# Attention's loads cut into pieces of 0.27 MB behind fixed places in TensorE's work, and row stores spread over several steps

## The chip, the cores and the metric

The kernel runs on one core of a Trainium2 chip. The metric is the device time of one execution, in microseconds (us). Before the change three runs gave a median of 729.78 us (729.25 to 739.17).

## The reference

Windowed attention with a few global tokens, followed by a mixture of experts in which a token may stay with the expert of the token before it. All data are fp32. Shapes: batch 8, 8 heads, 512 local and 32 global tokens, head size 64; 8 experts, 512 to 1024 to 512. Cut to what matters:

```python
# attention, for each batch and head
out_g = softmax(q_g @ [k_g, k_l].T / 8) @ [v_g, v_l]            # global tokens see all
s_ll  = where(|i - j| <= 32, q_l @ k_l.T / 8, -1e9)              # local tokens see a window
out_l = softmax([q_l @ k_g.T / 8, s_ll]) @ [v_g, v_l]            # and the global tokens
x = concat([out_g, out_l]) as [8, 576, 512]                      # heads side by side

# mixture of experts, for each batch b and token s in order
fresh = argmax(x[b, s] @ w_gate)
e = fresh if s == 0 or sigmoid(x[b, s] @ w_local) < 0.5 else e_of_the_token_before
p = softmax(x[b, s] @ w_gate)
out[b, s] = p[e] * (relu(x[b, s] @ w1[e]) @ w2[e])
```

## The kernel before

The program has two phases on one core. Attention comes first, in 48 steps; it writes each token's row (512 values, the 8 gate probabilities, the token's number) to a buffer `xs` in HBM. The experts follow: rows are gathered by expert, and two layers of matmuls run on blocks of 256 rows.

In attention a unit is either local, `l` (a pair of heads of one batch), or global, `g` (the global tokens of two pairs). A batch is six units: l, l, g, l, g, l. Step `s` does the scores of unit `s` (`l_s`, `l_max`, `l_exp`, or `g_s`, `g_max`, `g_exp`) and the rest of unit `s - 2`: `l_t` transposes the probabilities on TensorE and ScalarE copies them out of PSUM, `l_av` multiplies them with the values; `g_t` and `g_av` do the same for global units. A few pieces of a finished batch's routing (`f1` to `f3`) are put into later steps, and a list of small VectorE operations drips in between. The order of every engine's instructions is the order in which this code is written; nothing reorders it. In the program's lines: L240 are the local scores, L257 the transposes with the copies L259, L271 the products with the values; L291, L323 and L334 are the same for global units, L347 the transposes of `f1`, L370 a small product of `f2g`.

The loads of attention are issued on SyncE (SP), in order. One pair of heads needs one load of queries and keys (`qk`, 128 partitions, 528 KB) and one of values (`vw`, 128 partitions, 1040 KB), and a batch one small load of global queries (`qg`, 128 KB). The tiles come from rings: 8 for `qk`, 7 for `vw`. In the step of a local unit the kernel asks for the `qk` of the pair five ahead (AHEAD) and the `vw` of the pair four ahead (AHEADV). A load then waits on SP only until its tile is free, that is until the pair that was in it has been used, and everything behind it on SP waits too. GpSimd's `prep` builds a rearranged copy of a pair's keys one local unit ahead (L194).

A batch's rows are stored on ScalarE's queue (ACT) by `f4`, two steps after its routing is done: one store of 512 rows (`xa`, 1056 KB), four of the global tokens' rows (`xg`, 16 KB each) and one of their tail (`gx`, 2 KB), six issues in a row at the start of a step (L407, L411, L412). The stores of the seventh batch come behind the last step, those of the eighth in a list of work that runs beside the first experts' matmuls.

SP's and ACT's transfers share eight completion counters, which the order prints as DMAHW0 to DMAHW7: a transfer that takes a counter first waits for the transfer that had it before.

Four steps before the end of attention the experts' phase begins to work into it (`moe.pre`): the first rows are gathered, and the first expert weights are loaded on SP from step 45 on.

Of the kernel before, what the change touches and what calls it, by code (L numbers as in the profile page):

```python
# [18 lines left out]
P = 128  # L19
B, H, SL, SG, D = 8, 8, 512, 32, 64  # L20
# [34 lines left out]
RE = 2  # L55
XPM = (2, 4, 5, 6)
STORE = 2
AHEAD = 5
AHEADV = 4


def col(b):
# [38 lines left out]
class Attn:  # L101
    def __init__(self, tc, cst, tl, at1, at2, raw, ps, qk, qg, vw, xs):
        nc = self.nc = tc.nc
        self.tc, self.cst = tc, cst
        self.at1, self.at2 = at1, at2
        self.qk, self.qg, self.vw, self.xs = qk, qg, vw, xs
        self.ld = raw
        self.ps_s, self.ps_t, self.ps_o = ps
        self.xa = ring(tl, [P, 4, ROW], F32, "xa", 2)
        self.xa.t.append(at2.tile([P, 4, ROW], F32, name="xa2"))  # L110
        self.xg = ring(tl, [P, 2, D], F32, "xg", 3)
        self.xT = tl.tile([P, 4, SL], F32, name="xT")
# [12 lines left out]
        self.kx = ring(at2, [P, 9, 3, 32], F32, "kx", NBUF)  # L125
        self.pg = ring(at2, [P, 6, P], F32, "pg", NPG)
        self.ptg = ring(at2, [P, 6, P], F32, "ptg", 2)
        self.qgb = ring(at2, [P, NP, 2, 32], F32, "qgb", 2)
        self.mask = at2.tile([P, 4, 2, 32], BF16, name="mask")
        self.m0 = at2.tile([P, 2, 32], F32, name="m0")  # L130
        self.cur = {}
        self.stores = []
        self.s = 0
        self.gens = []
        self.low = 0
        self.banks = False
        self.npr = 0
# [28 lines left out]
    def setup(self):  # L166
# [5 lines left out]
        yield  # L172
        nc.sync.dma_start(self.xs[0:P], zr)

    def load(self, b, pr):
        nc = self.nc
        if pr == 0:
            self.cur[b] = {"v": []}
        c = self.cur[b]
        t = c[("qk", pr)] = self.ld()  # L180
        nc.sync.dma_start(t, self.qk[b, pr])

    def load_g(self, b):
        g = self.cur[b]["qg"] = self.qgb()
        self.nc.sync.dma_start(g, self.qg[b])

    def loadv(self, b, pr):
        nc = self.nc
        v = self.v()
        self.cur[b]["v"].append(v)  # L190
        nc.sync.dma_start(v.rearrange("p w c -> p (w c)"), self.vw[b, pr])

    def cp(self, out, in_, pat):
        self.nc.gpsimd.affine_select(out=out, in_=in_, pattern=pat, compare_op=ALU.is_ge, fill=0.0, base=0, channel_multiplier=0)  # L194
# [26 lines left out]
    def l_s(self, st):  # L221
        nc = self.nc
        b, pr = st["u"]
        if pr == 0:
            self.cur[b]["xa"] = self.xa()
            self.cur[b]["xg"] = self.xg()
        st["pe"] = self.pe()
        q = self.cur[b][("qk", pr)]
        kf = st["kx"].rearrange("p m c k -> p (m c k)")
        sp = st["sp"] = [self.bank(self.ps_s) for _ in range(2)]  # L230
        for h in range(2):
            mo = sp[h].rearrange("p t (k c) -> p t k c", c=32)[:, :, 0::3, :]
            nc.tensor.matmul(mo, self.cst.idb, self.mask, start=True, stop=False, skip_group_check=True)
        for t in range(4):
            for h in range(2):
                r = slice(64 * h, 64 * h + 64)
                for w4 in range(4):
                    w = 4 * t + w4
                    f = 32 * (3 * (w // 2) + w % 2)
                    nc.tensor.matmul(sp[h][32 * w4:32 * w4 + 32, t], q[r, 32 * w:32 * w + 32], kf[r, f:f + P], start=False, stop=True, skip_group_check=True)  # L240

    def l_max(self, st, h):
        nc = self.nc
# [9 lines left out]
    def l_t(self, st, hb):  # L253
        nc = self.nc
        tp = self.bank(self.ps_t)
        for i in range(4):
            nc.tensor.transpose(tp[:, i], st["pe"][:, 4 * hb + i], self.cst.idf)  # L257
        pt = self.pt()
        nc.scalar.copy(out=pt.rearrange("p t w q -> p t (w q)"), in_=tp)  # L259
        st["pts"] = st.get("pts", []) + [pt]  # L260

    def l_av(self, st, h):
        nc = self.nc
        b, pr = st["u"]
        c = self.cur[b]
        v = c["v"][pr]
        pt = st["pts"][h]
        o = self.ps_o()[:, 0:4 * (D + 1)].rearrange("p (t c) -> p t c", c=D + 1)
        for t in range(4):
            for w4 in range(4):  # L270
                nc.tensor.matmul(o[32 * w4:32 * w4 + 32, t], pt[:, t, w4, :],  # L271
                                 v[:, 4 * t + w4, h * (D + 1):(h + 1) * (D + 1)], start=True, stop=True, skip_group_check=True)
        rs = self.rs()
        nc.vector.tensor_scalar(out=rs, in0=o[:, :, D:D + 1], scalar1=1e-9, scalar2=None, op0=ALU.add)
        self.drip(hold=True)
        nc.vector.reciprocal(out=rs, in_=rs)
        self.drip(hold=True)
        n = D * (2 * pr + h)
        nc.vector.tensor_tensor(out=c["xa"][:, :, n:n + D], in0=o[:, :, 0:D], in1=rs.broadcast_to([P, 4, D]), op=ALU.mult)

    def g_s(self, st):
        nc = self.nc
        b, pp = st["u"]
        c = self.cur[b]
        st["sp"] = []
        for n0, n1 in ((0, 256), (256, 544)):
            sp = self.ps_s()
            for i in range(2):
                pr = 2 * pp + i
                k = c[("qk", pr)][:, SL:]  # L290
                nc.tensor.matmul(sp[64 * i:64 * i + 64, 0:n1 - n0], c["qg"][:, pr], k[:, n0:n1], start=True, stop=True, skip_group_check=True)  # L291
            st["sp"].append(sp[:, 0:n1 - n0])

    def g_max(self, st):
        nc = self.nc
# [21 lines left out]
    def g_t(self, st):  # L317
        nc = self.nc
        pt = st["pt"] = self.ptg()
        for c0 in (0, 3):  # L320
            tp = self.bank(self.ps_t)
            for i in range(3):
                nc.tensor.transpose(tp[:, i], st["pg"][:, c0 + i], self.cst.idf)  # L323
            nc.scalar.copy(out=pt[:, c0:c0 + 3], in_=tp[:, 0:3])

    def g_av(self, st):
        nc = self.nc
        b, pp = st["u"]
        c = self.cur[b]
        op = self.ps_o()  # L330
        for ci, w in enumerate(GCH):
            for i in range(4):
                pr, h = 2 * pp + i // 2, i % 2
                nc.tensor.matmul(op[32 * i:32 * i + 32, 0:D + 1], st["pt"][:, ci, 32 * i:32 * i + 32],  # L334
                                 c["v"][pr][:, w, h * (D + 1):(h + 1) * (D + 1)], start=(ci == 0), stop=(ci == 5), skip_group_check=True)
        rs = self.rsg()
        nc.vector.tensor_scalar(out=rs, in0=op[:, D:D + 1], scalar1=1e-9, scalar2=None, op0=ALU.add)
        self.drip(hold=True)
        nc.vector.reciprocal(out=rs, in_=rs)
        self.drip(hold=True)  # L340
        nc.vector.tensor_scalar(out=c["xg"][:, pp], in0=op[:, 0:D], scalar1=rs, scalar2=None, op0=ALU.mult)
# [58 lines left out]
    def f4(self, b, rt):  # L400
# [3 lines left out]
        hf, b4 = b // 4, b % 4  # L404
        rq = slice(32 * b4, 32 * b4 + 32)
        r0 = P * (1 + col(b))
        nc.scalar.dma_start(self.xs[r0:r0 + 4 * P].rearrange("(t p) r -> p t r", p=P), xa)  # L407
        r0 = P * (1 + gcol(hf)) + 32 * b4
        xsg = self.xs[r0:r0 + 32]
        for h in range(4):  # L410
            nc.scalar.dma_start(xsg[:, 0:DM].rearrange("q (a h d) -> q a h d", a=2, h=4)[:, :, h], xg[32 * h:32 * h + 32])  # L411
        nc.scalar.dma_start(xsg[:, DM:ROW], rt.gx[rq])  # L412

    def run(self, rt, moe):
        order = []
# [19 lines left out]
        for k in range(1, AHEAD):  # L435
# [3 lines left out]
                self.load_g(b)  # L439
            if k <= AHEADV:  # L440
                self.loadv(*pairs[k - 1]["u"])
        self.cst.ident()
        warm = self.ps_o()[:, 0:P]
        for _ in range(8):
# [8 lines left out]
        for s in range(n):  # L453
# [30 lines left out]
            else:  # L484
                self.g_s(nx)
                self.g_max(nx)
            fpiece()
            if nl:
                self.l_exp(nx, 0)
            else:  # L490
# [27 lines left out]
        self.drip(1000)  # L518
        for _, b in self.stores:
            self.f4(b, rt)  # L520
        moe.tail = self.tail(units[n - 2], units[n - 1], fin, rt, moe)

    def tail(self, sg, sl, fin, rt, moe):
# [32 lines left out]
        yield  # L556
        yield from rt.stage_b(self.ps_t, self.ps_o, rt.probs(b, c["L"], c["xa"]))
        self.f4(b, rt)
        yield from every(rt.lists(self.ps_o), 2)
        yield LISTS  # L560
        yield from every(rt.kinds(), 3)
# [1018 lines left out]
```

## Time and profile before

| | |
|---|---|
| median of three runs | 729.78 us |
| the profiled execution, a run of its own | 738.59 us |
| its span, first to last instruction | 736.9 us, mean granted TensorE clock 0.959 |
| scores of step 0 begin | 4.80 us |
| scores of the last step (47) begin | 262.76 us |
| the 48 steps and the flush behind them, to | 277.43 us |
| PE busy in 0 to 277 us | 219.61 us, clock 0.91 |
| DVE, ACT, POOL busy there | 182.53, 131.60, 58.76 us |
| bytes moved in those 277 us | 65.46 MB, mean 236 GB/s |

"PE" is TensorE's matmuls, "PEld" its weight loads, which overlap them; "DVE" is VectorE, "POOL" GpSimd, "SPq" and "ACTq" issues of transfers on the queues of SP and ACT. In a wait, the name behind the arrow is what the engine waited for last; "issue" means that nothing which the profile shows was missing.

### The profile page before, as it was taken

How to read it: one execution, taken by the hardware profiler on the slowest of the kernel's cores; microseconds unless marked ns; L12 is line 12 of the kernel's file. 1: busy time of each engine (PE TensorE's matmuls, PEld its weight loads, DVE VectorE, ACT ScalarE, POOL GpSimd, SP SyncE). 2: the span in 40 equal slices, each digit the busy share in tenths (PEclk: the TensorE clock that was granted, in tenths of full speed). 3: DMA queues.
4: the chain of work that ended last, by engine and by line, in shares of the span. 5: the costliest groups of instructions: out<-in, count | busy, mean ns of one | idle time of the engine just before them, and what ended most of it. 6: DMA issues, size and time to landing. Idle time of an engine off the chain costs nothing.

```text
span 736.9 us, 20404 instructions
## 1 busy us (share of the span) xinstructions
PE 661.8 (90%) x8277; PEld 551.8 (75%) x8277; DVE 422.4 (57%) x1052; ACT 343.9 (47%) x613; POOL 152.5 (21%) x259
## 2 busy tenths in 40 slices
PE   8689888687878869989899899999999999999996
PEld 6467656565656558779688788988888988988994
DVE  6566666655678666689732663533553634436563
ACT  4355545453545446464432753524353525345463
POOL 6112111121102130203121430304031202031122
PEclk9889989989989998999999999999999999999999
DMA  9976575847561455777662765725564725435763
GB/s 355 412 302 261 194 298 200 303 176 259 189 210 61 152 177 182 273 224 240 196 244 84 239 216 193 230 94 174 180 201 141 239 75 169 139 138 184 270 235 116
DMA packets 43019, 151.57 MB, mean 206 GB/s; under 512 B 7965, under 2 KB 9245, under 8 KB 38688
## 3 DMA queue, kind: packets, MB, share of 16 engines
q1 hardware_dynamic: 28368, 117.72, 45.5%
q0 software_dynamic: 6960, 21.90, 9.2%
q10 hardware_dynamic: 7456, 9.33, 3.7%
q8 instruction: 85, 1.39, 0.8%
q14 instruction: 150, 1.23, 0.5%
HBM read 130.55 MB, written 19.69 MB: 204 GB/s over the span
## 4 chain that ended last, share of the span: by engine, by line
PE 77%; DVE 10%; issue 5%; ACTq 3%; ACT 2%; DMA 1%; POOL 0%; DVEq 0%; POOLq 0%
PE ps L1270 27%; PE ps L1259 24%; PE ps L240 5%; PE ps L271 4%; PE ps L257 4%; PE ps L1212 3%; PE ps L347 2%; ACTq L411 2%; PE ps L291 2%; PE ps L334 2%; PE ps L323 2%; DMA xs<-xg 1%; DVE wp L1167 1%; DVE pe L247 1%; DVE mx L245 1%
## 5 line engine op out<-in xcount | busy, mean ns | idle before, releaser
L1270 PE MATMUL ps<-wp,wq 128*128 128x512 f32 x504 | 128.0, 401 | 1.0 <-ACT wq L1373 1.0
L1259 PE MATMUL ps<-wp,wp 128*128 128x256 f32 (+6 forms) x672 | 107.8, 320 | 1.5 <-issue 1.5
L1270 PEld LDWEIGHTS ps<-wp,wq 128*128 128x128 f32 x504 | 93.5, 190 | 20.8 <-ACT wq L1373 1.2
L1259 PEld LDWEIGHTS ps<-wp,wp 128*128 128x128 f32 x672 | 103.4, 189 | 5.5 <-issue 2.0
L1276 POOL DMA_INDIRECT out_dram<-y,tk x39 | 40.5, 1040 | 321.2 <-ACT y L1275 248.0
L1262 DVE SCALAR_TENSOR_TENSOR wq<-ps,wq 128x256 fp32r<-128x256 f32 (+6 forms) x80 | 41.3, 519 | 72.9 <-ACT wq L1261 65.2
L1261 ACT ACTIVATE wq<-ps 128x256 fp32r<-128x256 f32 (+6 forms) x80 | 36.8, 463 | 78.5 <-PE ps L1259 69.8
L1215 DVE TENSOR_TENSOR wp<-ps,wp 128x512 fp32r<-128x512 f32 x40 | 27.5, 691 | 79.7 <-ACT wp L1214 79.7
L245 DVE TENSOR_REDUCE mx<-ps 128x4 f32<-128x512 f32 x64 | 43.9, 685 | 36.4 <-PE ps L240 36.1
L1275 ACT ACTIVATE y<-ps,pp 128x512 f32<-128x512 f32 x39 | 26.9, 689 | 77.2 <-PE ps L1270 71.1
L251 ACT ACTIVATE pe<-pe 128x512 f32<-128x512 f32 x64 | 40.5, 633 | 40.8 <-DVE pe L247 40.3
L1167 DVE TENSOR_TENSOR wp<-raw,wp 128x1024 fp32r<-128x1024 f32 x47 | 56.9, 1217 | 2.8 <-ACT wp L1157 2.8
L1198 POOL DMA_INDIRECT xa<-xs,idx x42 | 51.3, 1221 | 17.1 <-issue 9.7
L259 ACT COPY pt<-ps 128x512 f32<-128x512 f32 x64 | 35.1, 595 | 40.3 <-DMA xs<-xg 17.7
L1157 ACT CAST wp<-raw 128x1024 fp32r<-128x1024 f32 x49 | 50.8, 1047 | 5.2 <-issue 3.8
L1214 ACT CAST wp<-ps 128x512 fp32r<-128x512 f32 x40 | 23.4, 590 | 55.2 <-PE ps L1212 55.2
L271 PE MATMUL ps<-v,pt 128*32 128x65 f32 x1536 | 31.4, 231 | 15.5 <-ACT pt L259 7.2
L247 DVE TENSOR_TENSOR pe<-ps,mx 128x512 f32<-128x512 f32 x64 | 44.1, 688 | 1.4
L1270 PE MATMUL ps<-hhl,wq 128*128 128x512 f32 x174 | 44.8, 398 | 0.0
L271 PEld LDWEIGHTS ps<-v,pt 128*32 128x32 f32 x1536 | 25.8, 115 | 25.1 <-ACT pt L259 10.4
L194 POOL TENSOR_SCALAR_AFFINE_SELECT kx<-raw 128x128 f32<-128x128 f32 (+1 forms) x64 | 21.9, 366 | 102.4 <-issue 76.9
L257 PE MATMUL ps<-idf,pe 128*128 128x128 f32 x256 | 39.9, 305 | 1.4 <-ACT pe L251 1.4
(284 smaller groups left out, 1168.5 us busy)
## 6 DMA issues: line engine op xcount, KB each, us to landing
raw<-in_w_dram SPq DMA_DIRECT2D x78, 512.0 KB, 4.1
v<-in_vw_dram SPq DMA_DIRECT2D x24, 1040.0 KB, 9.3
xa<-in_w_dram SPq DMA_DIRECT2D x26, 512.0 KB, 3.9
xT<-in_w_dram SPq DMA_DIRECT2D x20, 512.0 KB, 3.7
raw<-in_qk_dram SPq DMA_DIRECT2D x16, 528.0 KB, 6.5
xs<-xa ACTq DMA_DIRECT2D x8, 1056.0 KB, 7.4
hhl_a<-in_vw_dram SPq DMA_DIRECT2D x4, 1040.0 KB, 11.2
wp_a<-in_vw_dram SPq DMA_DIRECT2D x4, 1040.0 KB, 4.8
```

The costliest lines, as they stand in the source:

```text
L245: nc.vector.tensor_reduce(out=mx, in_=st["sp"][h], axis=AX.X, op=ALU.max)
L247: nc.vector.tensor_tensor(out=st["pe"][:, 4 * h:4 * h + 4], in0=st["sp"][h], in1=mx.broadcast_to([P, 4, P]), op=ALU.subtract)
L251: self.nc.scalar.activation(out=pe, in_=pe, func=AF.Exp, scale=SCALE)
L257: nc.tensor.transpose(tp[:, i], st["pe"][:, 4 * hb + i], self.cst.idf)
L271: nc.tensor.matmul(o[32 * w4:32 * w4 + 32, t], pt[:, t, w4, :], v[:, 4 * t + w4, h * (D + 1):(h + 1) * (D + 1)], start=True, stop=True, sk ...
L1157: nc.scalar.copy(out=hi, in_=raw)
L1167: (nc.gpsimd if pool else nc.vector).tensor_tensor(out=lo, in0=raw, in1=hi.bitcast(F32), op=ALU.subtract)
L1198: self.nc.gpsimd.indirect_dma_start(out=self.xr[j] if k == "early" else self.xr4[:, j], out_offset=None, in_=src, in_offset=bass.IndirectO ...
L1259: nc.tensor.matmul(ph, a[:, dc, fs], b_[:, dc, n0:n1], start=(n == 0), stop=(n == 11))
L1262: nc.vector.scalar_tensor_tensor(out=hl[:, fc, n0:n1], in0=ph, scalar=0.0, in1=hh[:, fc, n0:n1].bitcast(F32), op0=ALU.max, op1=ALU.subtract)
L1270: nc.tensor.matmul(py, a[:, fc, js], b_[:, fs], start=(fc == 0 and k == 0), stop=(fc == 7 and k == 2))
L1276: sc = nc.gpsimd.indirect_dma_start(out=self.out, out_offset=bass.IndirectOffsetOnAxis(ap=self.g[1][:, j:j + 1], axis=0), in_=y, in_offset ...
```

## The change

Loads. AHEAD and AHEADV go from 5 and 4 to 3 and 3. A load is no longer issued where it is asked for. `get` cuts it (`qk` into two pieces of 64 partitions, `vw` into four of 32 partitions, each some 0.27 MB; `qg` stays whole) and appends the pieces to a list, `due`. `pace` takes the first piece of the list and issues it on SP with a dependency on one instruction of TensorE, the last of a group: of `l_s`, of the second half of `l_t`, of each `l_av`, of each half of `g_s` and `g_t`, and of `g_av`. A piece then starts once that group is done. Before step 0 the pieces for the first three pairs are issued without such a dependency.

Stores. `f4` no longer issues but appends to a list, `puts`: `xa` as four stores of 128 rows, and the others as before, nine in all. `put(2)` issues two of them in each step, between the routing pieces and the exponential. What is left is issued behind the last step, and all nine at once for the last batch.

```diff
-AHEAD = 5
-AHEADV = 4
+AHEAD = 3
+AHEADV = 3
...
+    def get(self, to, of, n):
+        for k in range(0, P, n):
+            self.due.append((to[k:k + n], of[k:k + n]))
+
+    def pace(self, ins=None, n=1):
+        for _ in range(min(n, len(self.due))):
+            d = self.nc.sync.dma_start(*self.due.pop(0))
+            if ins is not None:
+                self.tc.add_manual_dep(d.ins, ins.ins.name, mybir.DependencyInfo(mybir.DependencyClass.Sync, mybir.DependencyReason.DATA), reason="pace")
+
     def load(self, b, pr):
...
-        nc.sync.dma_start(t, self.qk[b, pr])
+        self.get(t, self.qk[b, pr], 64)
...
-        self.nc.sync.dma_start(g, self.qg[b])
+        self.get(g.rearrange("p a h q -> p (a h q)"), self.qg[b], P)
...
-        nc.sync.dma_start(v.rearrange("p w c -> p (w c)"), self.vw[b, pr])
+        self.get(v.rearrange("p w c -> p (w c)"), self.vw[b, pr], 32)
...
-                    nc.tensor.matmul(sp[h][32 * w4:32 * w4 + 32, t], q[r, 32 * w:32 * w + 32], kf[r, f:f + P], start=False, stop=True, skip_group_check=True)
+                    i = nc.tensor.matmul(sp[h][32 * w4:32 * w4 + 32, t], q[r, 32 * w:32 * w + 32], kf[r, f:f + P], start=False, stop=True, skip_group_check=True)
+        self.pace(i)
...
+        if hb:
+            self.pace(x)
...
-        nc.scalar.dma_start(self.xs[r0:r0 + 4 * P].rearrange("(t p) r -> p t r", p=P), xa)
+        for t in range(4):
+            self.puts.append((self.xs[r0 + P * t:r0 + P * t + P], xa[:, t]))
...
-            nc.scalar.dma_start(xsg[:, 0:DM].rearrange("q (a h d) -> q a h d", a=2, h=4)[:, :, h], xg[32 * h:32 * h + 32])
-        nc.scalar.dma_start(xsg[:, DM:ROW], rt.gx[rq])
+            self.puts.append((xsg[:, 0:DM].rearrange("q (a h d) -> q a h d", a=2, h=4)[:, :, h], xg[32 * h:32 * h + 32]))
+        self.puts.append((xsg[:, DM:ROW], rt.gx[rq]))
+
+    def put(self, n):
+        for _ in range(min(n, len(self.puts))):
+            self.nc.scalar.dma_start(*self.puts.pop(0))
...
+        self.loadv(*pairs[AHEADV - 1]["u"])
+        self.pace(n=len(self.due))
...
             fpiece()
+            self.put(2)
...
         for _, b in self.stores:
             self.f4(b, rt)
+        self.pace(n=len(self.due))
+        self.put(len(self.puts))
...
         self.f4(b, rt)
+        self.put(len(self.puts))
```

The dependency of `pace` is set in the same way behind the other groups that the text names.

Where it stands on SP, for the loads of the third batch's first pairs (`hhl_a`, `wp_a`, `xhl_a` and `xr_a` are ring tiles that hold q/k or values at this time, `qgb` holds global queries, `v` values). Before:

```order
L181 DMA hhl_a<-in_qk_dram 128x1056 [waits DMAHW4_49,PE_49]
L185 DMA qgb_148<-in_qg_dram 128x256 [waits DMAHW5_49,PE_49]
L191 DMA v_130<-in_vw_dram 128x2080 [waits DMAHW6_49,PE_49]
L181 DMA wp_a<-in_qk_dram 128x1056 [waits DMAHW7_49]
L191 DMA v_131<-in_vw_dram 128x2080 [waits DMAHW0_49,PE_49]
L181 DMA xhl_a<-in_qk_dram 128x1056 [waits DMAHW1_49,Pool_49]
```

And in the changed kernel:

```order
L183 DMA hhl_a<-in_qk_dram 64x1056 [waits DMAHW5_49,PE_49]
L183 DMA hhl_a<-in_qk_dram 64x1056 [waits DMAHW6_49,PE_49]
L183 DMA qgb_148<-in_qg_dram 128x256 [waits DMAHW7_49,PE_49]
L183 DMA v_131<-in_vw_dram 32x2080 [waits DMAHW0_49,PE_49]
L183 DMA v_131<-in_vw_dram 32x2080 [waits DMAHW1_49,PE_49]
L183 DMA v_131<-in_vw_dram 32x2080 [waits DMAHW2_49,PE_49]
L183 DMA v_131<-in_vw_dram 32x2080 [waits DMAHW3_49,PE_49]
L183 DMA wp_a<-in_qk_dram 64x1056 [waits DMAHW4_49,PE_49]
L183 DMA wp_a<-in_qk_dram 64x1056 [waits DMAHW5_49,PE_49]
L183 DMA v_132<-in_vw_dram 32x2080 [waits DMAHW6_49,PE_49]
L183 DMA v_132<-in_vw_dram 32x2080 [waits DMAHW7_49,PE_49]
```

Each piece is an issue of its own now, waits for TensorE, and takes a counter; values are loaded one pair nearer to their use.

On ACT, at the store of the first batch's rows (`pg` are the exponentials of a global unit, `pt` the copies of transposes, `pe` the exponentials of a local unit). Before:

```order
L309 ACTIVATE pg_144<-ps_65,nb_124 128x32
L407 DMA xs<-xa_104 128x4x528 [waits DMAHW7_49]
L411 DMA xs<-xg_107 32x2x64 [waits DMAHW0_49]
L411 DMA xs<-xg_107 32x2x64 [waits DMAHW1_49]
L411 DMA xs<-xg_107 32x2x64 [waits DMAHW2_49]
L411 DMA xs<-xg_107 32x2x64 [waits DMAHW3_49]
L412 DMA xs<-gx 32x16 [waits DMAHW4_49]
L259 COPY pt_140<-ps_67 128x512 [waits PE_49,Activation_49]
L259 COPY pt_141<-ps_68 128x512 [waits PE_49,Activation_49]
```

And in the changed kernel:

```order
L272 COPY pt_140<-ps_67 128x512 [waits PE_49,Activation_49]
L272 COPY pt_141<-ps_68 128x512 [waits PE_49,Activation_49]
L380 COPY gsb<-ps_70 128x512 [waits DVE_49,PE_49]
L434 DMA xs<-xa_104 128x528 [waits DMAHW7_49]
L434 DMA xs<-xa_104 128x528 [waits DMAHW0_49]
L262 ACTIVATE pe_136<-pe_136 128x512 [waits DVE_49]
L340 COPY ptg_146<-ps_67 128x384 [waits PE_49]
L340 COPY ptg_146<-ps_68 128x384 [waits PE_49]
L262 ACTIVATE pe_136<-pe_136 128x512 [waits DVE_49]
L365 COPY xT<-ps_67 128x512 [waits PE_49]
L434 DMA xs<-xa_104 128x528 [waits DMAHW6_49]
L434 DMA xs<-xa_104 128x528 [waits DMAHW7_49]
```

The six issues that stood ahead of the copies `pt` have become pairs behind those copies, ahead of an exponential, in five steps (the first two of the five are shown).

More of the change, by code (lines that the diff above doesn't have):

```diff
@@ L132, in __init__ @@
         self.stores = []
+        self.due = []
+        self.puts = []
         self.s = 0
@@ L173, in setup @@
         nc.sync.dma_start(self.xs[0:P], zr)
+    def get(self, to, of, n):
[6 more added lines that the diff above has]
+                self.tc.add_manual_dep(d.ins, ins.ins.name, mybir.DependencyInfo(mybir.DependencyClass.Sync, mybir.DependencyReason.DATA), reason="pace")
     def load(self, b, pr):
-        nc = self.nc
         if pr == 0:
@@ L180, in load @@
         t = c[("qk", pr)] = self.ld()
-        nc.sync.dma_start(t, self.qk[b, pr])
+        self.get(t, self.qk[b, pr], 64)
     def load_g(self, b):
         g = self.cur[b]["qg"] = self.qgb()
-        self.nc.sync.dma_start(g, self.qg[b])
+        self.get(g.rearrange("p a h q -> p (a h q)"), self.qg[b], P)
     def loadv(self, b, pr):
-        nc = self.nc
         v = self.v()
         self.cur[b]["v"].append(v)
-        nc.sync.dma_start(v.rearrange("p w c -> p (w c)"), self.vw[b, pr])
+        self.get(v.rearrange("p w c -> p (w c)"), self.vw[b, pr], 32)
     def cp(self, out, in_, pat):
@@ L256, in l_t @@
         for i in range(4):
-            nc.tensor.transpose(tp[:, i], st["pe"][:, 4 * hb + i], self.cst.idf)
+            x = nc.tensor.transpose(tp[:, i], st["pe"][:, 4 * hb + i], self.cst.idf)
+        if hb:
+            self.pace(x)
         pt = self.pt()
@@ L270, in l_av @@
             for w4 in range(4):
-                nc.tensor.matmul(o[32 * w4:32 * w4 + 32, t], pt[:, t, w4, :],
-                                 v[:, 4 * t + w4, h * (D + 1):(h + 1) * (D + 1)], start=True, stop=True, skip_group_check=True)
+                i = nc.tensor.matmul(o[32 * w4:32 * w4 + 32, t], pt[:, t, w4, :],
+                                     v[:, 4 * t + w4, h * (D + 1):(h + 1) * (D + 1)], start=True, stop=True, skip_group_check=True)
+        self.pace(i)
         rs = self.rs()
@@ L290, in g_s @@
                 k = c[("qk", pr)][:, SL:]
-                nc.tensor.matmul(sp[64 * i:64 * i + 64, 0:n1 - n0], c["qg"][:, pr], k[:, n0:n1], start=True, stop=True, skip_group_check=True)
+                x = nc.tensor.matmul(sp[64 * i:64 * i + 64, 0:n1 - n0], c["qg"][:, pr], k[:, n0:n1], start=True, stop=True, skip_group_check=True)
             st["sp"].append(sp[:, 0:n1 - n0])
+            self.pace(x)
     def g_max(self, st):
@@ L322, in g_t @@
             for i in range(3):
-                nc.tensor.transpose(tp[:, i], st["pg"][:, c0 + i], self.cst.idf)
+                x = nc.tensor.transpose(tp[:, i], st["pg"][:, c0 + i], self.cst.idf)
+            self.pace(x)
             nc.scalar.copy(out=pt[:, c0:c0 + 3], in_=tp[:, 0:3])
@@ L333, in g_av @@
                 pr, h = 2 * pp + i // 2, i % 2
-                nc.tensor.matmul(op[32 * i:32 * i + 32, 0:D + 1], st["pt"][:, ci, 32 * i:32 * i + 32],
-                                 c["v"][pr][:, w, h * (D + 1):(h + 1) * (D + 1)], start=(ci == 0), stop=(ci == 5), skip_group_check=True)
+                x = nc.tensor.matmul(op[32 * i:32 * i + 32, 0:D + 1], st["pt"][:, ci, 32 * i:32 * i + 32],
+                                     c["v"][pr][:, w, h * (D + 1):(h + 1) * (D + 1)], start=(ci == 0), stop=(ci == 5), skip_group_check=True)
+        self.pace(x)
         rs = self.rsg()
```

## The prediction

> **What bounds the kernel now.** I read the page first, then the windows of attention batch by batch, then TensorE's waits there, then the timeline at single waits. The page shows how busy each engine is and, in forty slices, the DMA engines' share; the last line is the queue that brings instructions.
>
> ```profile
> PE 661.8 (90%) x8277; PEld 551.8 (75%) x8277; DVE 422.4 (57%) x1052; ACT 343.9 (47%) x613; POOL 152.5 (21%) x259
> DMA  9976575847561455777662765725564725435763
> q8 instruction: 85, 1.39, 0.8%
> ```
>
> TensorE (PE) is the bound: the last 350 us are nearly all matmul and the change doesn't touch them. The change works on the first 263 us, the 48 steps of attention. A step begins where the scores of its unit begin; these windows are one batch of six steps each (the last five steps). Columns: length, busy us of PE, weight loads, DVE, ACT, POOL, then the granted clock, the DMA share and GB/s.
>
> ```profile
> 4.80:30.23 25.43, 21.05 (x566) 15.08 (x566) 16.47 (x53) 11.48 (x27) 11.11 (x50) 0.93 1.02 413
> 30.23:63.70 33.47, 27.54 (x718) 20.69 (x717) 21.48 (x82) 16.66 (x37) 5.49 (x16) 0.90 0.72 285
> 63.70:93.88 30.18, 25.62 (x718) 19.19 (x717) 20.51 (x74) 16.17 (x37) 5.49 (x16) 0.94 0.71 258
> 93.88:127.55 33.67, 27.34 (x718) 19.84 (x717) 21.12 (x74) 16.48 (x37) 5.49 (x16) 0.90 0.64 232
> 127.55:161.83 34.28, 27.18 (x718) 19.84 (x716) 21.07 (x74) 16.35 (x37) 5.49 (x16) 0.90 0.65 228
> 161.83:200.02 38.19, 28.15 (x723) 20.84 (x722) 25.05 (x90) 16.91 (x39) 5.54 (x16) 0.91 0.68 248
> 200.02:235.77 35.75, 28.57 (x760) 21.80 (x758) 28.05 (x111) 15.92 (x37) 5.50 (x16) 0.90 0.43 151
> 235.77:262.76 26.99, 23.37 (x586) 16.84 (x585) 18.28 (x57) 15.02 (x35) 5.75 (x11) 0.94 0.40 129
> ```
>
> The same matmuls take 30 to 34 us per batch, at a clock of 0.90 to 0.94. The next windows are single steps with no or little idle time, one for each place in a batch: first, second, third, fourth, and fifth with sixth.
>
> ```profile
> 235.77:239.50 3.73, 3.73 (x128) 3.05 (x127) 2.51 (x7) 2.69 (x5) 2.10 (x5) 1.00 0.02 4
> 134.18:138.15 3.97, 3.97 (x142) 3.12 (x140) 3.69 (x12) 2.57 (x6) 1.37 (x4) 1.00 0.93 323
> 74.76:79.39 4.63, 3.93 (x92) 2.91 (x92) 4.23 (x15) 3.17 (x9) 0.00 (x0) 1.00 0.95 335
> 252.34:257.45 5.11, 4.86 (x152) 3.41 (x150) 3.54 (x10) 2.62 (x7) 0.00 (x0) 1.00 0.36 132
> 119.76:127.55 7.79, 7.79 (x215) 6.08 (x215) 5.90 (x25) 5.25 (x13) 1.37 (x4) 1.00 0.50 167
> ```
>
> They add to 25.23 us: an undisturbed batch, all at clock 1.00. The four ordinary batches (second to fifth) took 131.60, on average 32.90, so 7.67 us of each are disturbance. What disturbs is in PE's waits of the first 277 us (us in total, times, longest).
>
> ```profile
> PE ps L240 <- issue: 10.8, 7, 3.5
> PE ps L271 <- ACT pt L259: 7.2, 4, 2.7
> PE ps L334 <- issue: 6.0, 3, 3.7
> PE ps L271 <- issue: 5.3, 4, 2.2
> PE ps L354 <- ACT pt L259: 3.8, 2, 2.4
> PE ps L347 <- issue: 1.8, 1, 1.8
> PE ps L370 <- issue: 1.7, 1, 1.7
> PE ps L347 <- ACT pt L259: 1.5, 2, 0.8
> ```
>
> Two kinds: 25.6 us (10.8+6.0+5.3+1.8+1.7) put to "issue", and 12.5 us (7.2+3.8+1.5) of waiting for ACT's copy L259. The first kind in the timeline, with two windows that run from the end of one such wait to the end of a later one, and the window of the wait itself:
>
> ```profile
> 30.64 0.63 PE L240 MATMUL ps<-kx,raw 64*32 64x128 f32 x20
> 34.81 1.52 PE L240 MATMUL ps<-kx,raw 64*32 64x128 f32 x44 [3.54 <-issue]
> 34.80:46.97 12.17, 10.02 (x254) 7.45 (x254) 8.40 (x29) 5.33 (x10) 2.45 (x7) 0.86 1.02 413
> 98.78:105.75 6.97, 5.27 (x127) 3.95 (x127) 4.43 (x16) 2.70 (x5) 1.37 (x4) 0.76 0.67 252
> 31.27:34.81 3.54, 0.00 (x2) 0.00 (x1) 2.01 (x8) 0.72 (x2) 0.29 (x1) 0.99 1.02 403
> ```
>
> PE stops in the middle of one group of 64 score matmuls, where no operand is missing. Between such stops lie 127+127 = 254 instructions, or 508: always the same block. The instruction queue's packets are 1.39 MB / 85 = 16.4 KB. So I read these stops as PE waiting for its next block of code, and they fall where the DMA engines are saturated (1.02) by loads. [...]
>
> The second kind is the store of a batch's rows, on ACT's queue:
>
> ```profile
> 77.78 0.40 ACTq L407 DMA_DIRECT2D xs<-xa  x1
> 80.04 2.46 ACTq L411 DMA_DIRECT2D xs<-xg  x2
> 83.08 1.07 ACT L259 COPY pt<-ps 128x512 f32<-128x512 f32 x2 [3.93 <-DMA xs<-xg]
> 83.71 0.66 PE L271 MATMUL ps<-v,pt 128*32 128x65 f32 x32 [1.75 <-ACT pt L259]
> L411 ACTq DMA_DIRECT2D xs<-xg x32: 440/985/2177, 78.2 to 316.3; - x32
> ```
>
> Six issues in a row hold ACT for about 4 us, then PE waits for ACT. Their issue is 0.44 us at the least, 0.985 in the median.
>
> **The change part by part.** *Loads.* These rows give what one load or store moves (KB, us to landing), one issue on SP, and the last wait for a store.
>
> ```profile
> v<-in_vw_dram SPq DMA_DIRECT2D x24, 1040.0 KB, 9.3
> raw<-in_qk_dram SPq DMA_DIRECT2D x16, 528.0 KB, 6.5
> qgb<-in_qg_dram SPq DMA_DIRECT2D x8, 128.0 KB, 2.3
> xs<-xa ACTq DMA_DIRECT2D x8, 1056.0 KB, 7.4
> 73.87 0.33 SPq L191 DMA_DIRECT2D v<-in_vw_dram  x1
> 277.43 1.53 PE L334 MATMUL ps<-v,ptg 128*32 128x65 f32 x48 [6.33 <-ACT ptg L324]
> ```
>
> Per batch eight large loads become 24 pieces (4 pairs x (2+4)) and one small one. TensorE passes 26 places per batch (4 x 4 in local units, 2 x 5 in global ones), so 25 pieces fit, with one to spare; the first two steps lack places (no unit two steps back), which leaves a backlog of some ten pieces that shrinks by one a batch. SP issues 200 loads instead of 72: 128 x 0.33 = 42 us more, spread over 258 us on a queue that has nothing else to do: nothing. Behind a waiting piece on SP stand only later pieces and, from step 45, the first expert weights; the last pairs are asked for in step 42 and have gone out by 44, so nothing there either. Being only three pairs ahead is covered too: a pair is first touched by the prep of the step two pairs later, at least two steps or 8 us on, its two q/k pieces go first, and even 528 KB land in 6.5. Without that cover each late pair would cost PE up to 6.5 us.
>
> What it removes: a block of code now meets a piece of 0.27 MB ahead of it, not 1.04 + 0.53. The trace shows no such piece, so I bound what stays of the 7.67 us: nothing (as in the undisturbed rows, two of which had a DMA share of 0.93 and more), or all. I take 0.27/1.04 = a quarter, 1.9 us, since the waits come from what stands in the queue and the low clock comes after the waits. That gives 25.2 + 1.9 = 27.1 per batch.
>
> *Stores.* Nine issues instead of six per batch, two per step over five steps. At 0.40 to 0.44 each that is 0.9 us in a step in which ACT is busy for about 2.7 (16.4 / 6), and it stands ahead of an exponential that waits for DVE anyway: nothing. The 12.5 us and their share of the low clock go; they are within the 7.67. The store of the seventh batch is still flushed at once behind the last step (6.33 us in the last row above), and that of the eighth in the tail: no change.
>
> *Start.* q/k of the first pair comes in two issues; the first of them took 0.39, so I add 0.5 us.
>
> The sum, against the profiled execution's own 738.6 (span 736.9, and 1.7 around it):
> - ordinary batches: 131.6 - 4 x 27.1 = 23.2;
> - sixth: DVE has 25.05 against 21.05 on average in the ordinary ones, so 27.1 + 4.0 = 31.1, gain 7.1;
> - seventh: DVE 28.05, so 27.1 + 7.0 = 34.1, gain 1.6;
> - the last five steps: 25.2 - 3.9 + 1.6, and 1.8 for the MoE matmuls that PE already does there (23.37 us at clock 0.94 are 22.2, against 24.3 - 3.9 in the undisturbed rows): 24.7, gain 2.3;
> - the first batch: 25.43 already, gain 0; start -0.5.
>
> Together 33.7, so 704.9, 705. With nothing left of the disturbance it would be 692 (25.23 in place of 27.1), with all left 739. The profiled execution is 8.8 us above the median of the runs (729.78), whose own waits must have been fewer; the end point doesn't depend on them. What comes next on PE's heels is DVE: 21.05 of 27.1 us.
>
> **The rivals.**
> 1. *Half cured.* The same bytes in less time make the DMA engines busier, 0.70 to about 0.85, so a block often finds a piece, or two, ahead of it. For it: a clock of 0.76 in a window with a DMA share of 0.67. Against it: 134.18 to 138.15, without a wait at 0.93. With half of the 7.67 left, a batch is 29.1: 15.2 + 5.1 + 0 + 0.7 - 0.5 = 20.5, so 718.
> 2. *Pieces that move at half the rate.* All 128 partitions together reached 413 GB/s. Nothing here shows a load of 32 or 64 partitions; if it got half, 207, the 6.55 MB of a batch (4 x (528 + 1040) + 128 KB) would take 31.7 us and its stores 1.08 MB / 413 = 2.6 more, 34.3 per batch. 47 steps are 7.83 batches: 268.7 us where they now take 258.0, so 749 and slower. It turns against the change below about 216 GB/s, where a batch takes the present 32.9, and into slower by 2% below 211. For it: DMA is already at 0.65 to 0.72. Against it: no row; but pieces for different partitions can be under way together, up to eight. [...]
> 3. *The loads aren't the cause, or ACT is held after all.* Eight completion counters go round among SP's and ACT's transfers, so a store on ACT can wait for a piece that waits for TensorE. Then either kind of wait stays; with the 12.5 us gone alone, 726.
>
> **How the numbers follow.** Chances: 0.58 for the forecast (692 to 713), 0.19 for rival 1, 0.14 for rival 2, 0.09 for rival 3. The predicted time is 705. The range, 690 to 728, holds all but rival 2 and some 0.05 at the edges. About 2% (715 and 744 from the median) is what a measurement of this kernel can tell: faster 0.63 (forecast and a quarter of rival 1), slower 0.10 (most of rival 2), the rest 0.27 the same.
>
> **What would show it.** In the changed kernel's profile PE's waits put to "issue" in attention fall from 25.6 us to under 8, waits for L259's successor behind a store are gone, the clock of an ordinary batch rises from 0.90 or 0.94 to 0.96 or more, an ordinary batch takes 26 to 28 us, and DVE stays at 21. Pieces that land in over 5 us, or a DMA share of 1.0 at some 200 GB/s, would mean rival 2; long ACT issues of the stores, rival 3; code waits as before at a DMA share of 0.85, rival 1. Were PE to wait for v or q/k directly, the look-ahead would be too short and my cover wrong.

## The result and the profile after

The changed kernel takes 777.71 us in the median of three runs (777.25 to 783.92) against 729.78 before: 1.063 times as long, 95% interval 1.051 to 1.075. It is slower, and outside the predicted range. The profiled execution took 783.92 us, 1.8 of it around the span. Its page, with PE's line and the forty slices of the DMA engines' share and rate:

```profile
span 782.1 us, 20773 instructions
PE 684.6 (88%) x8277; PEld 569.0 (73%) x8277; DVE 420.6 (54%) x1052; ACT 346.2 (44%) x613; POOL 152.0 (19%) x259
DMA  9998859788977798586767267472638442517763
GB/s 198 211 216 192 192 144 204 202 196 210 217 190 169 190 237 213 192 287 209 248 221 270 82 221 241 164 242 77 217 118 268 157 168 79 192 63 253 244 239 119
```

In the first three slices the DMA engines have a share of 0.92 to 0.93 at 198 to 216 GB/s; before, the first two reached 355 and 412 at a share of nine tenths or more. The prediction named this as the mark of its second rival. The loss lies in attention alone: the scores of the last step begin at 309.7 us instead of 262.8, and the span is 45.2 us longer. Windows of the same batches as in the prediction, with the same columns, for the first, second, fifth and sixth:

```profile
4.81:44.27 39.46, 25.55 (x565) 17.91 (x565) 18.09 (x60) 12.10 (x28) 9.99 (x46) 0.83 0.98 217
44.27:80.39 36.12, 27.64 (x718) 20.25 (x717) 20.43 (x76) 16.06 (x36) 5.32 (x16) 0.86 0.88 203
152.05:188.93 36.88, 27.63 (x718) 20.17 (x717) 21.18 (x74) 16.83 (x38) 5.33 (x16) 0.91 0.84 205
188.93:233.90 44.97, 30.87 (x723) 22.61 (x722) 25.57 (x90) 17.49 (x39) 6.68 (x20) 0.82 0.85 199
```

The first batch, which I had at a gain of 0, alone takes 39.5 us instead of 25.4, at a DMA share of 0.98 and 217 GB/s. The waits in 0 to 325 us (total, times, longest), of PE, of POOL and of SP, each from its own view:

```profile
PE ps L250 <- POOL kx L204: 23.0, 18, 6.2
PE ps L250 <- issue: 14.5, 5, 4.7
PE ps L284 <- issue: 11.2, 7, 2.4
PE ps L305 <- DMA xr_a<-in_qk_dram: 7.4, 2, 6.3
```
```profile
POOL kx L204 <- DMA raw<-in_qk_dram: 113.1, 14, 16.4
```
```profile
SPq L183 <- DMA xs<-xa: 63.2, 16, 10.7
SPq L183 <- DMA xs<-xg: 49.6, 9, 9.0
SPq L183 <- DMA v<-in_vw_dram: 20.5, 26, 3.3
```

Read backwards, TensorE's scores (L250) wait for the rearranged keys, GpSimd's `prep` waits for q/k, and the q/k pieces come late. The waits put to "issue", which I read as waits for code, (14.5 + 11.2 us, 27.2 with the small ones) are as long as before (25.6). And SP, on which the pieces stand, waited 112.8 us for stores on ACT's queue, which the prediction had nowhere: 63.2 + 49.6. By the two pages, 22.8 of the 45.2 us are longer matmuls (PE 684.6 against 661.8 busy, at a mean clock of 0.923 against 0.959), and the rest is longer waiting.

So there were three suspects: the rate of pieces that touch 64 or 32 partitions (HALF RATE), the completion counters shared with the stores (COUNTERS), and a look-ahead of three pairs behind places in TensorE's work (LOOK-AHEAD).

### The profile page after: what moved, and what is told of

Read it like the earlier page. It is cut to its first block, busy times and chain, and to the rows that moved or that the text cites. A ratio compares the mean times of both kernels' runs of the same rounds, so it can differ in the third digit from the quotient of the medians.

```text
span 782.1 us, 20773 instructions
## 1 busy us (share of the span) xinstructions
PE 684.6 (88%) x8277; PEld 569.0 (73%) x8277; DVE 420.6 (54%) x1052; ACT 346.2 (44%) x613; POOL 152.0 (19%) x259
## 4 chain that ended last, share of the span: by engine, by line
PE 68%; DMA 15%; DVE 7%; issue 5%; ACT 2%; POOL 2%; SPq 1%; ACTq 1%; DVEq 0%; POOLq 0%
PE ps L1298 24%; PE ps L1287 22%; DMA raw<-in_qk_dram 4%; PE ps L250 4%; DMA v<-in_vw_dram 3%; PE ps L284 3%; PE ps L268 2%; PE ps L1240 2%; DMA xr_a<-in_qk_dram 2%; PE ps L305 2%; PE ps L364 2%; DMA xs<-xg 1%; PE ps L350 1%; DVE wp L1195 1%; POOL kx L204 1%
## 5 line engine op out<-in xcount | busy, mean ns | idle before, releaser
L284 PE MATMUL ps<-v,pt 128*32 128x65 f32 x1536 | 34.3, 240 | 17.3 <-issue 11.2
L284 PEld LDWEIGHTS ps<-v,pt 128*32 128x32 f32 x1536 | 28.1, 122 | 26.6 <-issue 17.8
L250 PE MATMUL ps<-kx,raw 64*32 64x128 f32 x1024 | 26.9, 323 | 21.5 <-POOL kx L204 13.6
```

Of the source, the lines that this page charges most:

```text
L250: i = nc.tensor.matmul(sp[h][32 * w4:32 * w4 + 32, t], q[r, 32 * w:32 * w + 32], kf[r, f:f + P], start=False, stop=True, skip_group_check= ...
L284: i = nc.tensor.matmul(o[32 * w4:32 * w4 + 32, t], pt[:, t, w4, :], v[:, 4 * t + w4, h * (D + 1):(h + 1) * (D + 1)], start=True, stop=True ...
```

## The experiments

Each kernel was timed beside the kernel before on one chip; the ratios are to that. The kernel before had medians of 734.81, 728.69, 732.39 and 730.6 us in the four groups.

**1. Four kernels that part the suspects.** Column pieces, changed against the changed kernel:

```diff
-        for k in range(0, P, n):
-            self.due.append((to[k:k + n], of[k:k + n]))
+        c = to.shape[1] * n // P
+        for k in range(0, to.shape[1], c):
+            self.due.append((to[:, k:k + c], of[:, k:k + c]))
```

> The changed kernel with one thing altered: a load is cut along its columns, over all 128 partitions (q/k in two pieces of 528 columns, v in four of 520), so number and size of the pieces, their places behind TensorE, their order on SP, their completion counters and the stores stay. Theory HALF RATE (pieces that touch 32 or 64 partitions move at about half of the 413 GB/s that whole loads reached): the rate comes back, the windowed DMA share falls to about 0.65 at 230 to 260 GB/s, TensorE's waits for POOL's prep go, and the time is 700 to 725. Theory COUNTERS (pieces on SP are held by the stores on ACT's queue with which they share completion counters): nothing changes, 770 to 785. Theory LOOK-AHEAD (three pairs ahead, each piece held behind a place in TensorE's work, is too late whatever the rate): nothing changes, 770 to 785.

Uncut loads behind the same places:

```diff
-        self.get(t, self.qk[b, pr], 64)
+        self.get(t, self.qk[b, pr], P)
...
-        self.get(v.rearrange("p w c -> p (w c)"), self.vw[b, pr], 32)
+        self.get(v.rearrange("p w c -> p (w c)"), self.vw[b, pr], P)
```

> The changed kernel with uncut loads (528 and 1040 KB on 128 partitions), still three pairs ahead, each behind one place in TensorE's work; stores as in the changed kernel. HALF RATE: 128 partitions per load again, so 705 to 735 (the upper end if the waits for code come back with the large loads). COUNTERS: loads still stand behind stores on shared counters, 755 to 780. LOOK-AHEAD: 765 to 785, TensorE still waits for prep, which waits for q/k.

Only the cutting, put into the kernel before (`cut` issues the pieces on the spot):

```diff
-        nc.sync.dma_start(t, self.qk[b, pr])
+        self.cut(t, self.qk[b, pr], 64)
...
-        nc.sync.dma_start(v.rearrange("p w c -> p (w c)"), self.vw[b, pr])
+        self.cut(v.rearrange("p w c -> p (w c)"), self.vw[b, pr], 32)
```

> The kernel before with one thing altered: the loads are cut along partitions as in the changed kernel (q/k 2 x 64, v 4 x 32), but issued where they are asked for, five and four pairs ahead, with the stores as before. HALF RATE: the pieces are slow here too; 6.55 MB of a batch at 200 to 230 GB/s are 28 to 33 us, with the stores beside them 31 to 36, so 740 to 770, with a DMA share of 0.9 to 1.0 at about 210 GB/s through attention. COUNTERS and LOOK-AHEAD: neither the nine stores nor the places are there, 725 to 738, like the kernel before.

Only the loads changed, `f4` issuing its six stores at once as before:

```diff
-        for t in range(4):
-            self.puts.append((self.xs[r0 + P * t:r0 + P * t + P], xa[:, t]))
+        self.nc.scalar.dma_start(self.xs[r0:r0 + 4 * P].rearrange("(t p) r -> p t r", p=P), xa)
```

> The changed kernel with the row stores as before (six in a row, at once) and only the loads changed. HALF RATE: 770 to 785, the loads set the time. COUNTERS: fewer stores between the pieces, each batch's stores once instead of over five steps, so SP's waits for stores fall from 112.8 us to under 40 and the time to 735 to 760. LOOK-AHEAD: 770 to 785.

Measured: columns 716.66 us (ratio 0.976, 0.968 to 0.984), whole 721.53 (0.985, 0.978 to 0.993), parts 821.87 (1.123, 1.115 to 1.130), old stores 817.29 (1.116, 1.109 to 1.124). LOOK-AHEAD falls: with the same places and three pairs, TensorE's waits for `prep` go from 23.0 us to 0.6 (columns) and none (whole loads). What is left in the kernel with columns, first lines of PE's waits:

```profile
PE ps L251 <- issue: 7.1, 5, 3.4
PE ps L351 <- ACT ptg L341: 6.6, 1, 6.6
PE ps L285 <- ACT pt L273: 5.0, 1, 5.0
```

The kernel with only the parts shows that being able to have many pieces under way doesn't help. Here nothing paces them; its slices in 20 to 240 us:

```profile
DMA  5999999999600069999940679999507999972449
GB/s 126 219 236 227 256 228 239 214 224 232 175 3 3 4 212 205 213 235 222 215 114 3 212 174 223 232 228 213 137 17 248 228 215 223 237 172 80 149 134 222
```

Where the share is 9 the rate is 205 to 256 GB/s, and then there are gaps with next to nothing under way. In a gap SP waits for stores:

```profile
SPq L177 <- DMA xs<-xg: 65.9, 4, 24.4
```

That is COUNTERS, beside the rate: a piece on SP waits up to 24.4 us for a store that ACT issues late, and behind it no other piece goes out. With the six stores in a row both kernels lie above every expectation. With old stores SP's waits for stores were to fall under 40 us by COUNTERS, and they were 89.6 in the first 325 us. The nine spread stores made the changed kernel better than its loads alone (777.7 against 817.3).

**2. Which partitions, and the parts of the gain.** Strided rows, to see whether it matters which partitions a piece holds, changed against the changed kernel:

```diff
-        for k in range(0, P, n):
-            self.due.append((to[k:k + n], of[k:k + n]))
+        m = P // n
+        for k in range(m):
+            self.due.append((to[k::m], of[k::m]))
```

> The changed kernel with other rows in each piece: a q/k piece is every second partition (0, 2, 4, ... and 1, 3, 5, ...), a v piece every fourth, so still 64 and 32 partitions with whole rows of 4224 and 8320 bytes, the same number, size, order, places and stores. [...] Theory COUNT (it matters how many rows a piece has: 64 or 32 rows for 16 DMA engines are too few, or too long): nothing changes against the changed kernel, 770 to 785.

Measured 736.70 us (1.009, 1.004 to 1.014). Every queue's order and every piece's counter is the same as in the changed kernel; only the rows differ, and 41 us are gone. SP's load queue in 20 to 240 us (packets, MB, share of 16 engines), of the kernel before, the changed one and this one:

```profile
q1 hardware_dynamic: 8969, 45.69, 55.7%
```
```profile
q1 hardware_dynamic: 9193, 38.48, 75.9%
```
```profile
q1 hardware_dynamic: 10764, 44.93, 63.0%
```

Bytes by busy time are 45.69 MB / (0.557 x 220 us) = 373 GB/s, 230, and 324. COUNT falls, for the pieces have as few and as long rows as before. But the time stayed 20 us above the columns (716.66). SP's waits here:

```profile
SPq L184 <- DMA xs<-xa: 70.1, 16, 10.2
SPq L184 <- DMA xs<-xg: 24.4, 7, 6.6
```

In the kernel with columns the pieces wait 1.9 us for stores. Its instructions on SP stand in the same order, but the program gives the counters out otherwise: in strided rows the first stores took counters 7, 0, 6, 7, 2, 3, in columns the four stores of `xa` took 3, 5, 3, 5. In both about as many of the 200 loads take a counter that a store had last (34 and 33), but in columns the first store comes 12 transfers later in the order of the counters, so the pieces that wait for it stand further back on SP. In the timeline of strided rows, first SP's issue of four pieces, then, from ACT's, the store issue that releases them:

```profile
67.87 13.42 SPq L184 DMA_DIRECT2D hhl_a<-in_vw_dram  x4
```
```profile
76.01 0.83 ACTq L435 DMA_DIRECT2D xs<-xa  x2
```

and of columns, the same four pieces:

```profile
70.52 2.99 SPq L184 DMA_DIRECT2D hhl_a<-in_vw_dram  x4
```

In the same group ran the stores' half of the change alone (loads issued whole where they are asked for, five and four pairs ahead), the loads' half alone with columns, and columns with the two stores per step issued on SP; for the last, `put` takes the queue:

```diff
-            self.put(2)
+            self.put(2, nc.sync)
```

> The kernel before with the change of the stores alone (nine, two per step; loads whole, at once, five and four pairs ahead). If the stores carry the gain that the column pieces showed: 710 to 720, with TensorE's waits for the copy behind a store (12.5 us) gone. If they carry only that and ACT's stores are held by whole loads on the shared counters: 725 to 738, with ACT waiting for DMA v or q/k in attention. By the prediction's terms (12.5 us gone, 25.6 us of waits put to issue still there): 717 to 727.

> The pieces along columns, paced as in the changed kernel, with the stores as before. If loads and stores add up, and the loads carry the larger share as predicted (a quarter of the code waits left): 715 to 725, waits put to issue under 12 us, waits for the copy behind a store some 12 us. If stores and paced pieces hold each other through the shared counters, as slow pieces and the stores before did (817 against 778): 735 to 760.

> Pieces along columns, and the two stores per step issued on SP in place of ACT, so that no store stands ahead of an exponential on ACT. With pieces along columns ACT still had two waits for v pieces ahead of an exponential (8.4 us in all, longest 5.7) and its store issues took it some 0.44 us each. If these are on the path: 705 to 713. If ACT's issues are hidden and only transfers count: 712 to 720, as with the stores on ACT (716.66). If stores ahead of pieces on SP delay the loads: 720 to 735, with TensorE waiting for POOL's prep.

Measured: stores alone 716.11 us (0.980, 0.972 to 0.987), column loads with old stores 730.96 (1.005, 1.001 to 1.009), columns with stores on SP 706.69 (0.968, 0.960 to 0.976; runs 705.81 to 710.15). With the stores spread on ACT, the gain is the stores' (0.980, against 0.976 with columns too): the copy behind a store no longer holds PE. PE's waits with stores alone, where those for code stay near what they were (all lines with "issue" together 21.2 against 25.6):

```profile
PE ps L249 <- issue: 8.0, 6, 2.8
PE ps L283 <- issue: 5.0, 8, 1.6
PE ps L349 <- issue: 4.7, 2, 2.4
PE ps L363 <- ACT pt L271: 1.6, 3, 0.8
```

and with column loads and old stores, where the code waits fall instead (10.1 us in all) and the copy takes their place. It was to cost some 12 us, as before, and cost 31.8 on three lines, of which the first is shown, so the time is neither of the two that were expected:

```profile
PE ps L285 <- ACT pt L273: 23.5, 5, 5.4
PE ps L251 <- issue: 5.0, 3, 2.6
PE ps L285 <- issue: 3.9, 3, 1.7
```

**3. Counters out of the way.** The last edit (steps' stores on SP, so that a piece's counter was last held by something ahead of it on SP) was put into four ways of loading.

> Pieces of every second or fourth partition as in the run with strided rows (736.7), and the two stores per step issued on SP in place of ACT, so that the counter that a piece waits for was last held by a transfer that stands ahead of it on SP itself. If the 20 us between strided rows and column pieces (716.66) are the shared counters (SP waited 94.5 us for stores there, and in the column pieces the counters fell otherwise): 703 to 713, as column pieces with stores on SP (706.69). If they are what is left of the rate (long rows, few per piece): 725 to 737.

> The changed kernel, its pieces of 64 and 32 neighbouring partitions kept, with the two stores per step issued on SP in place of ACT. If the rate of the pieces and the counters each cost their own, as the pair of strided runs would say: 745 to 760, loads at about 215 to 230 GB/s of busy share and SP without waits for stores on ACT. If the rate alone sets the time: 765 to 785. If the counters alone do: 705 to 720.

> Whole loads on 128 partitions, three pairs ahead and behind places in TensorE's work, with the two stores per step on SP. If the cutting has a worth of its own (shorter waits for code behind a piece of 0.27 MB than behind 1.04): slower than column pieces with stores on SP, 711 to 722. If not: 703 to 711.

> The kernel before, its loads whole, at once, five and four pairs ahead, with the nine stores of a batch two per step on SP. If only the stores' way mattered in the whole change: 703 to 712, and neither cutting nor pacing is worth anything. If stores behind loads that wait on SP for a free tile come too late or hold the loads: 715 to 735. If pacing or cutting has a worth of its own beside them: 712 to 720.

Measured: strided rows 710.54 us (0.973, 0.967 to 0.979), the changed kernel's neighbouring partitions 760.69 (1.039, 1.031 to 1.046), whole paced 721.92 (0.986, 0.979 to 0.993), whole at once 724.64 (0.992, 0.988 to 0.997). Counters and rate each have a price, and cutting has a worth, since whole paced loads stay 15 us above the columns (0.986 against 0.968 of the kernel before, so 13 by the ratios). The rate's 50 us (760.69 against 710.54) are clean of the counters, since in both programs every transfer has the same one; they can be followed in two profiles. The changed kernel with stores on SP, page and PE's waits:

```profile
span 761.5 us, 20787 instructions
PE 672.8 (88%) x8277; PEld 559.7 (74%) x8277; DVE 421.5 (55%) x1052; ACT 345.0 (45%) x613; POOL 151.8 (20%) x259
```
```profile
PE ps L284 <- issue: 26.0, 13, 3.9
PE ps L250 <- issue: 17.5, 7, 4.9
PE ps L305 <- DMA xr_a<-in_qk_dram: 5.8, 1, 5.8
```

and strided rows with stores on SP:

```profile
span 707.6 us, 20788 instructions
PE 648.3 (92%) x8277; PEld 542.5 (77%) x8277; DVE 421.8 (60%) x1052; ACT 344.2 (49%) x613; POOL 152.0 (21%) x259
```
```profile
PE ps L285 <- issue: 6.6, 8, 2.8
PE ps L251 <- issue: 6.3, 8, 1.3
```

With the smaller groups, the waits for code are 45.4 us against 16.0. Of the 53.9 us between the spans they make 29.4, and matmuls that take longer, at a mean clock of 0.939 against 0.983, 24.5 (672.8 - 648.3). Little is waiting for data, 8.4 us here and 5.5 there with `prep`: slow pieces keep the DMA engines full (the load queue alone has a share of 89.9% in 20 to 240 us, against 78.9% with strided rows), and, as I read it, the blocks of code come late behind them.

**4. SBUF or HBM.** Rows apart are also read from other places in HBM. Two kernels, with stores on SP, have the same instructions with the same counters, and pieces of 64, 32 and 32 neighbouring rows; they differ in the bounds, and what counts is the time of the second against the first:

```diff
-        for k0, k1 in ((0, 64), (64, 96), (96, 128)):
+        for k0, k1 in ((32, 96), (0, 32), (96, 128)):
             self.due.append((to[k0:k1], of[k0:k1]))
```

> The changed kernel with its steps' stores on SP, and each load, q/k and v alike, cut into three pieces: partitions 0 to 63, 64 to 95, 96 to 127 (64, 32 and 32 neighbouring rows). No piece reaches partitions on both sides of 64. If slow pieces are a matter of the partitions reached (all three stay below or above 64), as much as of neighbouring rows read from HBM: slow like the changed kernel with stores on SP (760.69), 745 to 770.

> The same kernel, instruction for instruction, with other bounds: partitions 32 to 95, 0 to 31, 96 to 127, again 64, 32 and 32 neighbouring rows of the same bytes, in the same number, places and counters. The first piece, half of the bytes, reaches 32 partitions on each side of 64. [...] Theory HBM SIDE (long contiguous reads of 32 or 64 neighbouring rows are slow, wherever they are written): no difference, within 6 us of it.

Measured 766.13 us (1.052, 1.047 to 1.056) and 739.62 (1.012, 1.004 to 1.020). SP's queue in 20 to 240 us, of the first and of the second:

```profile
q1 hardware_dynamic: 14068, 47.63, 91.9%
```
```profile
q1 hardware_dynamic: 15508, 51.05, 85.8%
```

That is 236 and 270 GB/s. With half of the bytes at 236 and half at the 327 of strided rows with stores on SP (56.74 MB at a share of 78.9%) it would be 1 / (0.5/236 + 0.5/327) = 274. HBM SIDE falls: the second kernel is 26.5 us faster, where it had at most 6, and its mean is near what it would be if the piece that reaches 32 partitions on each side of 64 moved at the whole rate. Of loads that are cut, the waits for code were the longer the lower the rate, but for the last two. With the stores on SP they sum to 49.4 us at 236 GB/s (bounds from 0), 45.4 at 240 (the changed kernel's pieces), 34.0 at 270 (bounds from 32), 16.0 at 327 (strided rows) and 13.2 at 321 (columns); uncut loads, at 340, keep 26.3.

All loads and stores in one table (median us, ratio):

| loads | stores in a row on ACT | two per step on ACT | two per step on SP |
|---|---|---|---|
| whole, at once | 729.78 (before) | 716.11, 0.980 | 724.64, 0.992 |
| whole, paced | not run | 721.53, 0.985 | 721.92, 0.986 |
| columns, paced | 730.96, 1.005 | 716.66, 0.976 | 706.69, 0.968 |
| strided rows, paced | not run | 736.70, 1.009 | 710.54, 0.973 |
| neighbouring partitions, paced | 817.29, 1.116 | 777.71, 1.063 (changed) | 760.69, 1.039 |
| neighbouring partitions, at once | 821.87, 1.123 | not run | not run |

## Why the prediction was wrong

**The step that failed: the price of a piece.** "What it removes: a block of code now meets a piece of 0.27 MB ahead of it" took bytes for time. It put 0.27 MB at a quarter of a whole load's price, though no row showed a piece of fewer than 128 partitions. The runs show 224 to 240 GB/s of busy time for neighbouring partitions against 324 to 373 for strided or whole ones. So the DMA share rose (0.84 to 0.98 in the windows shown) and the waits for code stayed (27.2 us against 25.6) instead of falling under 8.

Rival 2 had the slow pieces, with 0.14. What I held against it, that pieces for different partitions can be under way together, did not help: in the kernel with only the parts, where nothing paces them, they moved 224 GB/s. But rival 2's sum does not give the loss either: at 240 GB/s it is 6.55 / 0.240 + 2.6 = 29.9 us a batch, a gain, where the changed kernel with stores on SP took 36.4 at that rate (285.2 us for 47 steps, at a DMA share of 0.91 and a clock of 0.87). Its 749 came from 207 GB/s, half of 413, a term that no run shows: the pieces moved at 224 to 240. What it lacked, as the waits show, is the late code (45.4 us) and the lower clock (0.91 before).

Of the cuts by rows, with the stores on SP, bounds of 32 to 95 are faster than 0 to 63 (270 against 236 GB/s), and every second or fourth row is the fastest (327). The changed kernel's pieces moved at 230 / 373 = 0.62 of the rate of whole loads before. So the rate goes with the partitions that a piece holds; by what mechanism was not shown. The slow pieces deserved the larger chance.

**A second step, left out: SP's wait for a store.** "Behind a waiting piece on SP stand only later pieces" was right, but not what the piece itself waits for. Rival 3 saw the shared counters only from ACT's side. With the steps' stores on SP the changed kernel is 17 us faster (777.71 against 760.69) and strided rows 26 (736.70 against 710.54). That edit also takes the issues off ACT. Columns, whose pieces hardly waited for stores, gain 10 by it, so some 16 of the 26 are the counters'; how much of the 17 is theirs was not parted. In all, of the 71 us between the columns with stores on SP (706.69) and the changed kernel, 50 are the neighbouring partitions, 17 the stores on ACT, and 4 lie between columns and strided rows.

**Right, at the whole rate.** With columns and stores on SP, another kernel than the one predicted, the time is 706.69, near the forecast's 705. That is partly luck, since terms offset. Its last scores begin at 234.70 us instead of 262.76, a gain of 28.1 where the sum had 33.7; another 3.3 came behind attention, where it had none. And the sum starts from an execution 8.8 us above the median: against the 728.69 of its own group the kernel gains 22. Windows of its second, third, sixth and seventh batch:

```profile
30.66:59.37 28.71, 25.53 (x718) 19.27 (x717) 21.46 (x81) 16.45 (x37) 6.65 (x20) 0.94 0.81 261
59.37:87.12 27.75, 24.50 (x717) 18.36 (x716) 21.17 (x78) 16.15 (x37) 5.32 (x16) 1.00 0.91 299
143.84:173.41 29.57, 26.17 (x723) 19.17 (x723) 24.47 (x86) 16.94 (x39) 5.45 (x16) 0.95 0.87 284
173.41:211.14 37.73, 31.58 (x760) 24.33 (x759) 27.81 (x111) 16.01 (x37) 5.50 (x16) 0.82 0.66 202
```

The four ordinary batches run from 30.66 to 143.84, on average 28.3 where I had 27.1: of 7.67 us of disturbance 40% stay, not a quarter. The cutting itself halves the waits for code, from 26.3 us (whole paced loads, stores on SP) to 13.2. The sixth came to 29.6 (31.1 predicted), the seventh to 37.7 (34.1).

- The bound was read rightly: PE, stopped, as I read it, by late code when the DMA engines are full. The changed kernel with stores on SP shows it from the other side (45.4 us of such waits where the kernel before had 25.6). That they would fall under 8 was too much: columns keep 13.4 (13.2 with stores on SP), strided rows 9.1 (16.0).
- The cover of three pairs holds at the whole rate (whole and column loads: at most 0.6 us of waits for `prep`; strided rows with stores on SP: one wait of 5.0 for q/k), and nearly so at the slow rate with the stores on SP (8.4 us for q/k, v and `prep`, the longest 5.8). The 23.0 + 7.4 us in the changed kernel came when both met.
- Spreading the stores did what was said, the 12.5 us of waiting for the copy went to 1.8 (stores alone). That ACT's nine issues cost nothing is not settled: columns gain 10 us when the stores leave ACT, but with whole paced loads the time stays (721.5 and 721.9).
- The start cost nothing: the first scores begin at 4.81 us instead of 4.80, where I had 0.5 us more.
- A slip without weight: in the last five steps, 23.37 us at a clock of 0.94 are 22.0, not 22.2.

What stays open is how the 10 us of the columns divide between ACT's issues and the counters, and why whole loads at once do worse with the stores on SP (724.64) than on ACT (716.11); loads that wait there for a free tile would hold the stores behind them, but that was not tried apart.

## What to carry to other kernels

Cut a load along its columns, which keeps all partitions in each piece, or take every second or fourth row; pieces of 32 or 64 neighbouring partitions below or above 64 moved at about 0.6 to 0.7 of the rate here (230 to 240 against 324 to 373 GB/s), and in the kernel with only the parts, where nothing paced them, no faster (224). Before transfers of two queues are interleaved, look up which completion counter each waits for: here SP, paced by TensorE, waited 112.8 us in the changed kernel for stores that ACT issued late. The fastest version here is the change with column pieces and the steps' stores on SP, 706.69 us.

## What the hardware showed unexpectedly

With the stores on SP the slow pieces took little from TensorE as missing data (8.4 us) and much as missing code, as I read the waits put to "issue": 45.4 us, single waits up to 4.9. Where the pieces were issued at once the code waits were 58.9 us within the first 300 us, single ones up to 7.1. No view names code as what was waited for; what speaks for it is the distance. In the changed kernel with stores on SP the first eight of these stops lie 127, 128, 128, 380, 380, 378 and 254 matmuls apart, the block of 127 that the prediction saw, or a multiple of it.

Attention's 5486 matmuls are some 43 such blocks. Before the change 16 waits were put to "issue" there, with strided rows and stores on ACT 8 (9.1 us, the least sum of all), and with neighbouring partitions and stores on SP 22. By number, then, 27 of 43 showed no wait before the change, and about half with the slow pieces.

The granted clock was lower where the waits were long, but did not follow them closely: over the whole run it is 0.983 with strided rows and stores on SP (16.0 us of code waits) and 0.976 with columns (13.2). Attention as one window, of the changed kernel and of columns with stores on SP:

```profile
4.81:309.72 304.91, 230.87 (x5486) 169.75 (x5486) 173.33 (x605) 126.10 (x282) 49.87 (x157) 0.83 0.84 199
```
```profile
4.81:234.70 229.89, 199.15 (x5486) 149.74 (x5486) 171.33 (x604) 124.40 (x283) 48.84 (x156) 0.95 0.83 269
```

The same 5486 matmuls take 230.87 us at a clock of 0.83 and 199.15 at 0.95; the DMA share is the same, 0.84 and 0.83, so the share alone doesn't set the clock. What lowers it was not tried.
